# Making the first residual load of GpSimd wait for the first inverse rows

## The chip, the cores and the metric

One core of one Trainium2 chip. The metric is the device time of the kernel in microseconds, launch to end; a traced execution also has a span, about 1.8 us shorter. Two executions of the kernel before were in a slower state (207.19 us in the first set of runs, 206.88 us in a later one) and are left out where fast runs are compared.

## The reference

```python
xn = layernorm(x)                                   # x: 1 x 2048 x 640, bfloat16
s  = irfft2(rfft2(xn) * (w_r + 1j * w_i))           # spectral filter over rows and columns
g  = silu((gelu(xn @ w_gate) * (xn @ w_up)) @ w_down)   # inner width 1536
out = x + s * g
```

The last line matters here: it adds x again, the *residual*, at the very end, when the x that was loaded at the start has been overwritten.

## The kernel before

The kernel is one long list of tasks that a planner in Python puts in order for each engine before the program is built. TensorE carries both halves: the transforms as matmuls, and the gated network, whose matmuls fill the gaps while the spectral data goes through DRAM. Each engine takes its list in order (VectorE's 320 and ScalarE's 224 operations come in one order in every trace whose lists are the same), and waits come only from data dependencies. Four parts matter.

The forward rows. Two slabs of rows at a time (a pair j, of eight) are transformed, evicted by ScalarE into a tile `mc`, which has two buffers, and stored to DRAM:

```python
BUFS = dict(..., mc=2, ..., xr=3, ...)
...
def cp(e, s=s, pa=pa):
    if s == 0:
        place(A, (2, D))                              # A is a buffer of mc
    copy_on(e, A.tile[:, s, :], flat(pa.tile)[:, 0:D])
...
stored[j] = dma(lambda: D2[:, 2 * j:2 * j + 2, :], lambda: A.tile, (0, -1, j), 327680, after=outs, ...)
```

The gate, whose GELU shares ScalarE's queue with those evictions, and whose PSUM bank `pg` (two of them) is free for TensorE only after it:

```python
nc.scalar.activation(out=ge.tile, in_=pg.tile ..., func=ACT.Gelu_apprx_tanh)
```

The residual loads, 16 of 160 KB, issued by GpSimd into a tile `xr` with three buffers:

```python
def load_res(n1):
    sx = Slot("xr")

    def go(e):
        place(sx, (D,))
        nc.gpsimd.dma_start(out=sx.tile, in_=xv[:, n1, :])
    xr_in[n1] = sx, add(go, "POOL", (600, 600), (5, n1), after=[y_done[n1]], new=[sx], size=163840)
```

And their only reader, VectorE, at the end of each slab: `res = yg + xr`, in the trace the operation `res<-yg,xr`.

`after=[y_done[n1]]` is a statement to the planner only. The load does not touch the inverse rows `y`, so no wait is built for it: on the chip it goes out as soon as GpSimd gets there and a buffer of `xr` is free.

## Time and profile before

| | before |
|---|---|
| median, three runs | 204.23 us (203.73 to 207.19) |
| span of the trace | 202.6 us |
| TensorE busy | 195.1 us, 96% |
| first three residual loads | issued at 48.69 us, first used at 154.97 us |
| store of the sixth pair of forward rows | issued at 50.60 us, ScalarE released at 57.88 us |

In the timelines below a line is: start in us, duration in us, engine, line of the program, operation, output<-input, shapes, count, and in brackets the idle time before it and what ended it. Such lines are taken from ScalarE's and TensorE's timelines of the kernel before:

```profile
57.88 1.29 ACT L296 CAST mc<-sp 128x640 bf16<-128x640 f32 x2 [4.82 <-DMA D<-mc]
...
59.72 1.24 PE L886 MATMUL pg<-xnT,Wg 128*128 128x512 bf16 x5 [1.35 <-ACT ge L903]
```

The two evictions stand idle for 4.82 us until the store out of their buffer is done, and the gate matmuls behind them in turn for 1.35 us.

TensorE's order is the same in all versions (its 1527 weight loads come in the same order in every trace). From the start of its last forward matmul to the start of its first spectral one lie the same instructions, and the stop lies in between:

```profile
52.54 0.38 PE L532 MATMUL sp<-mb,F1T 128*128 128x512 bf16 x1
...
67.28 1.06 PE L670 MATMUL sp<-T,BU 128*128 128x128 bf16 x16
```

I call 67.28 - 52.54 = 14.74 us stretch 1. In the same way stretch 2 goes from there to the first inverse matmul (78.03 us), and stretch 3 from there to the last block of inverse matmuls (43.59 us). What remains at the end, from the last VectorE operation to the end of the program, I call the tail (2.7 us; it is given to a tenth, as the span is).

### The profile page before, as it was taken

How to read it: one execution, taken by the hardware profiler on the slowest of the kernel's cores; microseconds unless marked ns; L12 is line 12 of the kernel's file. 1: busy time of each engine (PE TensorE's matmuls, PEld its weight loads, DVE VectorE, ACT ScalarE, POOL GpSimd, SP SyncE). 2: the span in 40 equal slices, each digit the busy share in tenths (PEclk: the TensorE clock that was granted, in tenths of full speed). 3: DMA queues.
4: the chain of work that ended last, by engine and by line, in shares of the span. 5: the costliest groups of instructions: out<-in, count | busy, mean ns of one | idle time of the engine just before them, and what ended most of it. 6: DMA issues, size and time to landing. Idle time of an engine off the chain costs nothing.

```text
span 202.6 us, 4105 instructions
## 1 busy us (share of the span) xinstructions
PE 195.1 (96%) x1509; PEld 117.9 (58%) x1527; DVE 149.6 (74%) x320; ACT 127.0 (63%) x224; POOL 33.0 (16%) x72
## 2 busy tenths in 40 slices
PE   7999999999979999999999999999999999999992
PEld 2994444666534646677755555467765555556771
DVE  3689979999323229999998999942247798888774
ACT  4898997965343567778766775433366666766421
POOL 2413347598000000000000000000001122111210
PEclk9999999999999999999999999999999999999998
DMA  6999999569966968643243201106800333323431
GB/s 178 328 316 326 347 391 231 119 160 222 178 246 198 345 183 233 138 122 113 68 130 104 96 5 60 68 13 218 351 3 32 99 119 110 98 100 97 129 102 65
DMA packets 35894, 32.62 MB, mean 161 GB/s; under 512 B 10910, under 2 KB 32930, under 8 KB 35874
## 3 DMA queue, kind: packets, MB, share of 16 engines
q1 hardware_dynamic: 34434, 29.49, 49.2%
q0 software_dynamic: 1152, 2.66, 5.3%
q10 hardware_dynamic: 288, 0.20, 0.5%
q8 instruction: 12, 0.20, 0.4%
q14 instruction: 8, 0.07, 0.1%
HBM read 22.51 MB, written 9.19 MB: 156 GB/s over the span
## 4 chain that ended last, share of the span: by engine, by line
PE 92%; DMA 4%; issue 1%; ACT 1%; DVE 1%; DVEq 0%; ACTq 0%
PE pu L886 24%; PE pg L886 23%; PE pg L968 13%; PE pu L968 12%; DMA D<-mc 4%; PE sp L697 3%; PE sp L830 3%; PE sp L772 2%; PE sp L806 2%; PE sp L368 2%; PE sp L670 2%; PE sp L532 1%; PE sp L690 1%; PE sp L824 1%; PE sp L463 1%
## 5 line engine op out<-in xcount | busy, mean ns | idle before, releaser
L886 PE MATMUL pg<-xnT,Wg 128*128 128x512 bf16 (+1 forms) x235 | 56.2, 365 | 1.8 <-ACT ge L903 1.4
L886 PE MATMUL pu<-xnT,Wu 128*128 128x512 bf16 (+1 forms) x237 | 57.2, 365 | 0.5
L907 DVE TENSOR_TENSOR uT<-pu,ge 128x512 bf16<-128x512 f32 x46 | 31.6, 689 | 22.6 <-PE pu L886 15.3
L968 PEld LDWEIGHTS <-uT 128*128 128x128 bf16 x396 | 37.8, 98 | 13.6
L903 ACT ACTIVATE ge<-pg 128x512 bf16<-128x512 f32 x46 | 27.3, 597 | 23.3 <-PE pg L886 22.4
L886 PEld LDWEIGHTS <-Wg 128*128 128x128 bf16 x285 | 25.5, 99 | 23.6 <-issue 1.6
L886 PEld LDWEIGHTS <-Wu 128*128 128x128 bf16 x285 | 25.1, 98 | 21.8
L931 POOL DMA_DIRECT2D xr<-in_A_x_dram x16 | 8.8, 551 | 135.7 <-DVE res L955 135.7
L968 PE MATMUL pg<-Wd,uT 128*128 128x320 bf16 (+2 forms) x204 | 30.5, 293 | 0.0
L968 PE MATMUL pu<-Wd,uT 128*128 128x320 bf16 (+1 forms) x192 | 29.7, 297 | 0.0
L296 ACT CAST ma<-sp 128x644 bf16<-128x644 f32 (+1 forms) x32 | 23.4, 793 | 9.7 <-PE sp L830 7.9
L296 ACT CAST mc<-sp 128x640 bf16<-128x640 f32 x15 | 9.8, 694 | 6.1 <-DMA D<-mc 4.8
L296 ACT CAST IU<-sp 128x640 bf16<-128x640 f32 x16 | 10.9, 691 | 4.2 <-PE sp L772 4.1
L977 ACT ACTIVATE th<-pg 128x320 f32<-128x320 f32 (+2 forms) x17 | 7.3, 427 | 9.9 <-PE pg L968 8.9
L296 ACT CAST Vt<-sp 128x640 bf16<-128x640 f32 x16 | 10.8, 691 | 3.7 <-PE sp L806 3.7
L982 DVE SCALAR_TENSOR_TENSOR G<-th,pg 128x320 bf16<-128x320 f32 (+1 forms) x16 | 7.6, 478 | 7.1 <-ACT th L977 6.9
L977 ACT ACTIVATE th<-pu 128x320 f32<-128x320 f32 (+1 forms) x16 | 7.0, 438 | 9.2 <-PE pu L968 9.0
L982 DVE SCALAR_TENSOR_TENSOR G<-th,pu 128x320 bf16<-128x320 f32 (+1 forms) x16 | 7.7, 479 | 5.6 <-ACT th L977 5.3
L433 POOL TENSOR_TENSOR RSTD<-MVA,mh 128x1 f32<-128x1 f32 x12 | 8.7, 729 | 4.0 <-DVE MVA L415 3.2
L848 DVE TENSOR_TENSOR mb<-ma 128x640 bf16<-128x640 bf16 x8 | 3.9, 493 | 7.0 <-ACT ma L296 7.0
L750 DVE TENSOR_TENSOR R<-Y 64x644 bf16<-64x644 bf16 x16 | 7.8, 490 | 0.4
L418 ACT ACTIVATE th<-X 128x640 bf16<-128x640 bf16 x11 | 8.1, 732 | 0.0
(106 smaller groups left out, 245.7 us busy)
## 6 DMA issues: line engine op xcount, KB each, us to landing
BU<-D SPq DMA_DIRECT2D x8, 640.0 KB
D<-mc SPq DMA_DIRECT2D x8, 320.0 KB
xr<-in_A_x_dram POOLq DMA_DIRECT2D x16, 160.0 KB, 2.6
D<-IU SPq DMA_DIRECT2D x8, 320.0 KB
out_dram<-res SPq DMA_DIRECT2D x15, 160.0 KB
Wg<-in_B_w_gate_dram SPq DMA_DIRECT2D x6, 320.0 KB
Wu<-in_B_w_up_dram SPq DMA_DIRECT2D x6, 320.0 KB
Wd<-in_B_w_down_dram SPq DMA_DIRECT2D x6, 320.0 KB
```

The source lines that it names most:

```text
L296: return nc.scalar.copy(out=out, in_=in_) if e == "ACT" else nc.vector.tensor_copy(out=out, in_=in_)
L418: nc.scalar.activation(out=place(junk, (D,)), in_=x, func=ACT.Copy, scale=-1.0 / D, accum_out=less)
L433: nc.gpsimd.tensor_tensor(out=rstd, in0=var, in1=mh, op=ALU.pow)
L697: nc.tensor.matmul(into(q, ri), lhsT=sZ.tile[:, q, ri, :], rhs=FM[:, kinds[q][2] + (4 if ri and kind == 0 else 0), :], start=False, stop=T ...
L750: nc.vector.tensor_tensor(out=o, in0=Yf[:, ::-3, :], in1=Yf[:, 1:3, :], op=ALU.subtract)
L886: nc.tensor.matmul(ps.tile[:, lo:hi + more], lhsT=w[:, c, t * P:(t + 1) * P], rhs=XR[:, c, lo + (lo > 0):hi + 1 if lo or more else hi] if ...
L903: nc.scalar.activation(out=ge.tile, in_=pg.tile if src is None else src, func=ACT.Gelu_apprx_tanh)
L907: nc.vector.tensor_tensor(out=u.tile, in0=pu.tile if src is None else src, in1=ge.tile, op=ALU.mult)
L931: nc.gpsimd.dma_start(out=sx.tile, in_=xv[:, n1, :])
L968: nc.tensor.matmul(ps.tile[:, 0:hi - lo], lhsT=uT[grp, ks[i]].tile[:, j * P:(j + 1) * P], rhs=Wd[:, ks[i], lo:hi], start=(i == 0), stop=(i ...
L977: nc.scalar.activation(out=th.tile[:, 0:hi - lo], in_=ps.tile[:, 0:hi - lo], func=ACT.Tanh, scale=0.5)
L982: nc.vector.scalar_tensor_tensor(out=G2.tile[:, lo:hi], in0=th.tile[:, 0:hi - lo], scalar=1.0, in1=ps.tile[:, 0:hi - lo], op0=ALU.add, op1 ...
```

## The change

Its intent is to keep the three early loads out of the busy time of the DMA engines. One element of the first inverse rows is copied into the buffer that the load will overwrite. The copy has to wait for those rows, the load has to wait for the copy, and GpSimd holds all later loads behind them (after the change they start at 151.02 us and later).

```diff
         def go(e):
             place(sx, (D,))
+            if n1 == 0:
+                nc.gpsimd.tensor_copy(out=sx.tile[0:1, 0:1], in_=y_of[0].tile[0:1, 0, 0:1])
             nc.gpsimd.dma_start(out=sx.tile, in_=xv[:, n1, :])
-        xr_in[n1] = sx, add(go, "POOL", (600, 600), (5, n1), after=[y_done[n1]], new=[sx], size=163840)
+        xr_in[n1] = sx, add(go, "POOL", (600, 600), (5, n1), after=[y_done[n1]], new=[sx], use=[] if n1 else [y_of[0]], size=163840)
```

## The prediction

> **What bounds the kernel now.** I read the page first. TensorE is busy 195.1 of 202.6 us, at a granted clock of nine tenths or more in every slice but the last, so the program is bound by its matmuls and a change can win only what TensorE still idles, about 7.5 us, or lose by making it idle more.
>
> ```profile
> PE 195.1 (96%) x1509; PEld 117.9 (58%) x1527; DVE 149.6 (74%) x320; ACT 127.0 (63%) x224; POOL 33.0 (16%) x72
> L931 POOL DMA_DIRECT2D xr<-in_A_x_dram x16 | 8.8, 551 | 135.7 <-DVE res L955 135.7
> L296 ACT CAST mc<-sp 128x640 bf16<-128x640 f32 x15 | 9.8, 694 | 6.1 <-DMA D<-mc 4.8
> ```
>
> The second line is the group that the change touches: 16 residual loads of GpSimd. It idles 135.7 us ahead of them, which costs nothing in itself. The third line says where a transfer stops an engine: ScalarE waits once, for 4.8 us, for a store out of the tile mc.
>
> Next, the view of TensorE's waits, to place its idle time. Only two are left: 1.2 us at the very start, for the dummy operand of the warm-up, and this one:
>
> ```profile
> PE pg L886 <- ACT ge L903: 1.4, 1, 1.4
> ```
>
> With the 4.0 us after the last matmul at 198.6 us, which no load of row 0 touches, these make 6.6 of the 7.5 us. So 1.4 us is the only large item in the body. Next, the chain of waits between 46 and 62 us, to see what made it (columns: start, duration, what):
>
> ```profile
> 50.30 0.29 ACT mc L296
> 50.60 7.21 DMA D<-mc
> ...
> 58.47 0.70 ACT mc L296
> 59.17 0.51 ACT ge L903
> 59.68 0.04 issue
> 59.72 1.24 PE pg L886 x5
> ```
>
> The store of the sixth pair of forward rows is issued at 50.60 and takes 7.21 us. The tile mc has two buffers, so ScalarE cannot evict the eighth pair before this store has landed; ScalarE is in order, so the GELU behind those two evictions waits too, and TensorE runs out of free gate banks. It stops from 58.37 to 59.72, 1.35 us. Landing to restart takes 59.72 - 57.88 = 1.84 us, so TensorE would not stop at all if the store landed at 58.37 - 1.84 = 56.53 or sooner, that is 1.35 us earlier (landing read as the 57.88 at which ScalarE resumes).
>
> Last, GpSimd in time and the DMA queues. The first line is GpSimd's timeline, the next ones the queue's shares of the 16 engines between 52 and 53 us and between 52 and 56 us:
>
> ```profile
> 48.69 1.72 POOL L931 DMA_DIRECT2D xr<-in_A_x_dram  x3
> ...
> 155.75 0.55 POOL L931 DMA_DIRECT2D xr<-in_A_x_dram  x1 [105.35 <-DVE res L955]
> ```
>
> ```profile
> q0 software_dynamic: 87, 0.33, 107.9%
> q1 hardware_dynamic: 156, 0.03, 18.6%
> ```
>
> ```profile
> q0 software_dynamic: 149, 0.49, 56.0%
> q1 hardware_dynamic: 875, 0.35, 53.8%
> ```
>
> Three residual loads, as many as xr has buffers, start at 48.69 although their rows are first used at 154.97, 106 us later. They move 480 KB on the software queue q0, exactly in the stretch in which the store waits behind two transposes on the hardware queue q1. Between 52 and 53 us q0 has practically all engines and q1 hardly moves.
>
> **What the Trainium skill says.** The page "DMA: Bandwidth & Descriptors", section "Queues, rings and completion order", says that each DMA engine takes turns between the queue rows that have work, packet by packet. The trace agrees: q0 has 56.0% and q1 53.8% of the engines over the same 4 us. The same page, section "Anatomy of one DMA — SWDGE (gpsimd) path", gives a load issued by GpSimd as about 2.0 us plus bytes/436e3; for 163,840 bytes that is 2.4 us, and the trace has 2.6 us for the undisturbed loads from 155 us on, but 4.9 to 7.3 us for the first three: they were in a crowd. The page "Perfetto Trace Analysis", section "Tensor Engine Instruction (MATMUL, LD_WEIGHTS)", says that GpSimd is strictly first in, first out; the loads of rows 1 and 2 therefore stay behind that of row 0.
>
> **The change part by part.**
>
> It *adds* one GpSimd copy of one element, once. The trace has no such copy; the shortest GpSimd instructions on tiny operands are 0.10 us (fills) and 0.19 us (128x1 scalar), spaced about 0.28 us to the next dependent one, so I count 0.3 us. GpSimd has nothing to do then: cost 0.
>
> It *adds a wait*: the copy reads column 0 of the first inverse rows, so it waits for VectorE's third inverse step (L856, which ends at 151.39 + 0.49 = 151.88) or, should the dependency cover the whole tile, for the fourth (L859, 152.54 + 0.48 = 153.02). The load needs the copy because both write the same buffer.
>
> It *moves* three loads, 480 KB, from 48.69 us to about 152 us. What they free early: 56.0% of 4 us is 2.24 us of all 16 engines. Had the engines been full throughout, the store would land 2.2 us earlier. They were not: between 54.5 and 56 us the DMA rate is low and the transposes' own tail sets the pace. The full stretch from 52 to 53 us is certain, the rest partly. So 1.0 to 2.2 us, in the middle 1.6 us. TensorE can use 1.35 us at the most. I count 1.25 us.
>
> What they cost late: the wake-up after VectorE's end is about 0.29 us (res ends 155.46, GpSimd's next load 155.75). Load 0 would then be issued at 151.88 + 0.29 + 0.3 = 152.5 and land 2.6 us later at 155.1, against 154.97 when VectorE wants it: a wait of about 0.1 us. With the later release it is 153.02 + 0.6 + 2.6 = 156.2: VectorE waits 1.25 us. DMA traffic is zero between 150 and 155 us, so nothing slows these loads. Rows 1 and 2 come 0.55 us apart and are wanted at 156.66 and 162.84, so they hold nothing up for long. Does a 1.25 us stop of VectorE reach TensorE? VectorE's next up-projection product starts at 157.71; before it stand four operations of 0.4 us, so it slips to about 157.9. The bank it frees is next written by TensorE at 162.15. VectorE idles 1.4 us of each 5.8 us period (0.79, 0.17 and 0.42), so the slip is gone one period later. Cost 0.
>
> Sum: 204.23 - 1.25 = 203.0 us.
>
> **Rivals.** *Everything hidden anyway.* If the store's landing depends on the transposes rather than on engine share, removing the 480 KB brings less than 0.5 us. For it: the low DMA rate after 54.5 us. Against it: q1's small share from 52 to 53 us, at 2 us of backlog. It would give about 203.8 to 204.2 us.
>
> *The wait takes the place of the one removed.* If GpSimd's wake-up or the load were much slower (5 us or more, as in the crowd of 50 us), VectorE would hold back products for long enough to stop TensorE; 0.5 to 2 us lost, 204 to 205 us. Against it: the DMA engines are idle there and TensorE has over 3 us in hand on the bank.
>
> *A larger gain.* If the next stage, which waits for all eight stores, also started earlier in a way that TensorE feels: but TensorE shows no wait between 59.72 us and its last matmul, so it could win only fractions of the remaining 0.9 us of small gaps: 202.3 us at best.
>
> **Range and chances.** The centre is 203.0. The full gain with some small gaps closed and a lucky run gives 202.2; no gain and a median as high as that before gives 204.3. Two per cent is 4.1 us, three times the whole idle time that this change can reach, and a loss of that size would need a stop of TensorE that no step above produces. So faster 0.02, same 0.96, slower 0.02. The kernel before had one run of 207.19 among three, so a stray slow run can move a median of few runs; this is most of the 0.02 for slower.
>
> **What would show each step.** Right: GpSimd's first load starts near 151 us, after a copy; between 52 and 56 us q0 is nearly empty; the store issued near 50.6 us takes about 5.6 us instead of 7.21; ScalarE's wait for it falls from 4.8 to about 3.2 us; TensorE's wait for ge falls from 1.4 us to almost none; VectorE shows a new wait of 0.1 to 1.3 us for the load xr near 154 us, and TensorE none behind it. Wrong: the store still lands near 57.8 us; or it lands earlier and TensorE stops somewhere else, for another transfer or for VectorE after 150 us.

## The result, and the profile after

| | before | after |
|---|---|---|
| median of six runs | 204.65 us (203.73 to 207.19) | 202.78 us (202.59 to 203.32) |
| fast runs, ratio | | 0.992 (95%: 0.9894 to 0.9945) |
| span of the trace | 202.6 us | 201.1 us |
| stretch 1, 2, 3 | 14.74, 78.03, 43.59 us | 13.22, 78.03, 43.60 us |
| tail | 2.7 us | 2.7 us |
| store: issue to ScalarE's release | 7.28 us | 3.42 us |

A ratio is the mean time of one kernel's fast runs over the mean time of the other's in the same rounds, so it is not quite the ratio of the medians. The gain in these runs is 0.8%, clear of noise and within the two per cent that count as "same". The kernels further down that hold the loads back and add nothing near 50 us gain 0.4 to 0.7% over the kernel before of their own group.

The page of the kernel after: TensorE has the same work in less time, GpSimd's load group has a copy ahead of it, and ScalarE's evictions into mc idle for 2.3 us in all, no longer mostly for the store.

```profile
PE 195.2 (97%) x1527; PEld 117.4 (58%) x1527; DVE 149.7 (74%) x320; ACT 127.2 (63%) x224; POOL 33.1 (16%) x73
L932 POOL COPY xr<-s 1x1 bf16<-1x1 bf16 x1 | 0.2, 182 | 101.8 <-DVE s L856 101.8
L296 ACT CAST mc<-sp 128x640 bf16<-128x640 f32 x15 | 9.8, 694 | 2.3 <-PE sp L533 1.3
```

(The kernel before shows 1509 matmuls and this one 1527. Each of the 18 missing records leaves a hole of about 0.05 us, 0.9 us in all, which is why its "idle" adds up to more than its stops.)

Timelines of ScalarE and TensorE after: the evictions wait 0.96 us instead of 4.82, the gate matmuls that had stopped start at 58.28 without a wait, and stretch 1 is 65.83 - 52.61 = 13.22 us.

```profile
54.10 1.29 ACT L296 CAST mc<-sp 128x640 bf16<-128x640 f32 x2 [0.96 <-DMA D<-mc]
```

```profile
52.61 0.38 PE L532 MATMUL sp<-mb,F1T 128*128 128x512 bf16 x1
...
58.28 1.24 PE L886 MATMUL pg<-xnT,Wg 128*128 128x512 bf16 x5
...
65.83 1.06 PE L670 MATMUL sp<-T,BU 128*128 128x128 bf16 x16
```

GpSimd's timeline after: the copy starts right after VectorE's third inverse step (149.95 + 0.49 = 150.44 us), the first load half a microsecond later.

```profile
150.50 0.18 POOL L932 COPY xr<-s 1x1 bf16<-1x1 bf16 x1 [101.75 <-DVE s L856]
151.02 0.59 POOL L933 DMA_DIRECT2D xr<-in_A_x_dram  x1 [0.34 <-POOL xr L932]
```

VectorE's timeline after has its first residual addition at 153.67 us, right behind the product that ends at 152.92 + 0.69 = 153.61. The load had landed at 153.55 us (151.02 + 2.5). From the start of the product to the start of the addition it is 0.75 us, and was 154.97 - 154.37 = 0.60 us in the kernel before: VectorE waited about 0.15 us for the load, too little for the views to show as idle time.

```profile
152.92 0.69 DVE L907 TENSOR_TENSOR uT<-pu,ge 128x512 bf16<-128x512 f32 x1 [0.42 <-PE pu L886]
153.67 0.49 DVE L957 TENSOR_TENSOR res<-yg,xr 128x640 bf16<-128x640 bf16 x1
```

The queues after, between 52 and 53 us (packets, MB, share of 16 engines): the hardware queue alone, at full share, where it had 18.6% before.

```profile
q1 hardware_dynamic: 345, 0.35, 111.9%
```

### The profile page after: what moved, and what is told of

Same layout as the page of the kernel before. It is cut to its first block, busy times and chain, and to the rows that moved or that the text cites.

```text
span 201.1 us, 4125 instructions
## 1 busy us (share of the span) xinstructions
PE 195.2 (97%) x1527; PEld 117.4 (58%) x1527; DVE 149.7 (74%) x320; ACT 127.2 (63%) x224; POOL 33.1 (16%) x73
## 4 chain that ended last, share of the span: by engine, by line
PE 79%; DMA 10%; SPq 4%; DVE 3%; issue 1%; ACT 1%; DVEq 0%
PE pg L886 19%; PE pu L886 19%; PE pg L970 13%; PE pu L970 12%; DMA X<-in_A_x_dram 6%; SPq L303 4%; DMA RB<-D 4%; PE sp L697 3%; PE sp L830 3%; PE sp L772 2%; PE sp L806 2%; PE sp L670 2%; PE sp L532 1%; PE sp L690 1%; PE sp L824 1%
## 5 line engine op out<-in xcount | busy, mean ns | idle before, releaser
L886 PE MATMUL pg<-xnT,Wg 128*128 128x512 bf16 (+1 forms) x245 | 57.5, 366 | 0.0
L903 ACT ACTIVATE ge<-pg 128x512 bf16<-128x512 f32 x46 | 27.4, 597 | 25.5 <-PE pg L886 25.0
L886 PEld LDWEIGHTS <-Wu 128*128 128x128 bf16 x285 | 25.1, 98 | 21.8
```

The lines of the kernel that those rows point to most:

```text
L886: nc.tensor.matmul(ps.tile[:, lo:hi + more], lhsT=w[:, c, t * P:(t + 1) * P], rhs=XR[:, c, lo + (lo > 0):hi + 1 if lo or more else hi] if ...
L903: nc.scalar.activation(out=ge.tile, in_=pg.tile if src is None else src, func=ACT.Gelu_apprx_tanh)
```

## The experiments

Theory A: the 480 KB of early residual loads slow the store out of `mc`, and through mc buffer, ScalarE and gate bank they stop TensorE; nothing else about the change matters. Twelve kernels ran, in three groups on three chips, each group beside its own runs of the kernel before, whose medians were 203.88, 204.38 and 204.37 us; so across groups it is ratios that compare. All twelve gave the right result. "Store" is from its issue to ScalarE's release, "VectorE" its longest wait for the residual rows (0: none that the views show).

| run | store | stretch 1 | stretch 3 | tail | VectorE | median | ratio to before |
|---|---|---|---|---|---|---|---|
| e1_copy_only | 5.97 | 13.22 | 43.60 | 2.7 | 0 | 203.56 | 0.9991 (0.9953 to 1.0029) |
| e2_dummy3 | 3.05 | 13.22 | 43.59 | 2.7 | 0 | 202.75 | 0.9958 (0.9923 to 0.9992) |
| e2_dummy1 | 3.95 | 13.22 | 43.59 | 2.7 | 0 | 202.86 | 0.9960 (0.9929 to 0.9991) |
| e4_before_mc3 | no wait | 13.50 | 43.60 | 2.7 | 0 | 203.10 | 0.9964 (0.9939 to 0.9990) |
| e3_early1 | 3.69 | 13.22 | 43.60 | 3.1 | 0.4 | 203.36 | 0.9956 (0.9921 to 0.9992) |
| e3_early2 | 5.02 | 13.23 | 43.59 | 3.1 | 0 | 203.53 | 0.9971 (0.9935 to 1.0007) |
| e3_early3 | 6.36 | 13.69 | 43.59 | 3.1 | 0 | 204.47 | 1.0007 (0.9972 to 1.0042) |
| e7_chain3 | 3.19 | 13.22 | 45.03 | 2.7 | 6.2 | 204.29 | 1.0000 (0.9957 to 1.0042) |
| e6_wait_zt | 3.24 | 13.22 | 43.59 | 2.7 | 0 | 202.83 | 0.9933 (0.9883 to 0.9983) |
| e8_col639 | 3.47 | 13.22 | 43.59 | 2.7 | 1.4 | 202.94 | 0.9946 (0.9910 to 0.9982) |
| e10_sp3_behind | 3.43 | 13.22 | 43.60 | 3.4 | 0 | 203.67 | 0.9977 (0.9942 to 1.0011) |
| e11_zt_mc3 | no wait | 13.22 | 43.59 | 2.7 | 0 | 202.78 | 0.9935 (0.9905 to 0.9966) |

Stretch 2 was 78.02 to 78.04 us in every one. The stretches and waits are from one traced execution each, the medians from four or six.

**e1_copy_only: the copy without the wait.**

```diff
-nc.gpsimd.tensor_copy(out=sx.tile[0:1, 0:1], in_=y_of[0].tile[0:1, 0, 0:1])
+nc.gpsimd.tensor_copy(out=sx.tile[0:1, 0:1], in_=ident[0:1, 0:1])
```

> The copy stays, its wait goes: it reads the identity matrix, ready since 1.5 us, so GpSimd's three loads go out at about 49 us as before. Theory A (the 480 KB in the crowd of 48 to 58 us are the whole cause): as the kernel before, the store out of mc takes about 7.2 us, TensorE waits about 1.4 us for ge, ratio to before 0.998 to 1.002. Rival B (the added instruction or its dependence on the buffer reorders something, and the traffic is hidden): as the changed kernel, ratio 0.992, no wait of TensorE for ge near 58 us.

The ratio is 0.9991: no gain from the copy in itself is seen. But the traced execution, at 203.01 us the fastest of its four (up to 204.55), shows no stop of TensorE at all, with the store at 5.97 us. So the stop is not there in every execution; how often it is, the record does not say, as each kernel has one trace (that the kernel before is about 1.6 us slower in the mean than the changed one suggests a stop in most). The limit of the prediction explains it: the kernel before would not have stopped had ScalarE been released by 56.53 us, which is 3.99 us after its last forward matmul at 52.54. Here that matmul was at 52.73, the limit is 56.72, and the release came just inside it:

```profile
56.55 1.29 ACT L296 CAST mc<-sp 128x640 bf16<-128x640 f32 x2 [3.29 <-DMA D<-mc]
```

**e2_dummy3 and e2_dummy1: dummy loads that missed their moment.** The changed kernel with three (one) more loads ahead of the copy, into the memory of a table that is loaded only at 75 us.

```diff
             if n1 == 0:
+                for i in range(3):
+                    nc.gpsimd.dma_start(out=flat(TI)[:, i * D:i * D + D], in_=xv[:, i, :])
                 nc.gpsimd.tensor_copy(...)
```

> The changed kernel with three dummy loads of the same 160 KB each, from the same rows, issued by GpSimd at the old moment into a tile that is still unused then; the real loads keep their wait. Theory A: the stop comes back, TensorE waits about 1.4 us, store near 7.2 us, ratio to before 0.998 to 1.002. Rival B (what helps is the later moment of the real loads, for buffers or VectorE): ratio 0.992.

> The same with one dummy load of 160 KB. Theory A with a cost in proportion to bytes: the store, 3.4 us without them and 7.2 us with three, takes about 4.7 us, it lands before TensorE's limit of 56.5 us, no wait of TensorE, ratio 0.992. Rival C (any load of the software queue stalls the transposes, whatever its size): the store takes 6 us or more and TensorE waits 0.5 to 1.4 us, ratio 0.995 to 1.0.

These did not test what they were to test: this place in the program comes after the readers of the table, so the dummies waited for them and ran at 100 to 133 us. They serve as a control. Up to 480 KB more through GpSimd, at a quiet time, cost nothing: stretch 2, in which they ran, is 78.03 us in both, and the medians are 202.75 and 202.86 us. (The ratios are 0.996 because this group's kernel before was faster. The trace of e2_dummy3 is the slowest of its four, 203.83 us; its extra 1 us lies before stretch 1, whose first matmul starts at 53.57 us.)

**e4_before_mc3: cure the wait, leave the loads.** The kernel before, with the eighth pair evicted into the memory of that table instead of the second mc buffer. (A real third buffer does not fit into SBUF: with `mc=3` the program does not build.)

```diff
-                if s == 0:
+                if s == 0 and j == 7:
+                    A.tile = flat(TI)[:, 0:2 * D].rearrange("p (s d) -> p s d", s=2)
+                elif s == 0:
                     place(A, (2, D))
```

> The kernel before, loads where they were, with the eighth pair of forward rows evicted into a third buffer (the memory of a table that is loaded only at 75 us) instead of the second mc buffer. Theory A with the chain store, mc buffer, ScalarE, gate bank, TensorE: ScalarE no longer waits for the store, TensorE's wait of 1.4 us is gone though the store still takes about 7 us; ratio 0.992 to 0.994. Rival D (the load traffic reaches TensorE by another way too, or the late store delays the next stage): ratio 0.996 to 1.0, with a new wait of TensorE near 60 to 68 us.

ScalarE's wait for the store and TensorE's wait for the bank are gone, which shows that the path through the mc buffer is real. But stretch 1 is 13.50, not 13.22 us. The loads are still in the crowd, the stores land late, and the regrouped rows that the spectral stage reads are issued only at 62.12 us (before: 61.49; after the change: 57.70). TensorE now waits for them, seen in the timeline of its weight loads:

```profile
66.33 0.73 PEld L672 LDWEIGHTS <-BU 128*128 128x128 bf16 x13 [0.60 <-DMA BU<-D]
```

So rival D is right in part: behind the first path stands a second one, shorter in what it costs (13.50 - 13.22 = 0.28 us), which emptying the crowd also clears.

**e3_early1, e3_early2, e3_early3: the traffic put back, in doses.** The changed kernel, with one, two or three dummy loads issued by GpSimd at the old moment, this time ahead of the table's own load.

```diff
-lambda e, ri=ri, w=w: nc.gpsimd.dma_start(out=D4[15:16, 1, ri, L:LP], in_=w[0:1, 0:1])
+lambda e, ri=ri, w=w: [nc.gpsimd.dma_start(out=D4[15:16, 1, ri, L:LP], in_=w[0:1, 0:1])]
+    + [nc.gpsimd.dma_start(out=flat(TI)[:, i * D:i * D + D], in_=xv[:, i, :]) for i in range(3 * ri)]
```

> One dummy load of 160 KB at about 48.7 us. Theory A with cost in proportion to bytes: store out of mc 4.3 to 5 us (3.4 without, 6 to 7.2 with three), lands before TensorE's limit, no stop, ratio 0.992 to 0.995. Rival C (any load of the software queue in this stretch upsets the transposes): store 6 us or more, TensorE stops in part, ratio 0.996 to 1.0.

> Two dummy loads at about 48.7 us; the store out of mc released ScalarE at 54.1 us with none of them, 54.5 with one, 57.1 with three. Theory A with a cost that grows faster than the bytes (two loads overlap with more of the transposes): release at 55 to 56.5 us, just ahead of TensorE's limit, no stop or a small one, the stretch of TensorE from the last forward matmul to the first spectral one 13.2 to 13.4 us (13.22 without a stop, 13.69 with three loads in their profile, 14.74 in the kernel before); ratio 0.993 to 0.998. Rival (proportional): release at 54.8 to 55.2 us.

> The three dummy loads of e2_dummy3, now put into the program ahead of the table's own load, so that GpSimd issues them at about 48.7 us (in e2_dummy3 they waited for the table's readers and ran at 100 to 133 us, which cost nothing). The real loads keep the wait. Theory A (bytes in the crowd): software queue busy between 51 and 56 us again, the store out of mc takes 6 to 7.5 us, ScalarE waits 3 to 5 us for it, TensorE stops for up to 1.5 us; ratio to before 0.997 to 1.002. Rival B (the later moment of the real loads is what helps): ratio 0.992 to 0.995, no stop.

The store took 3.69, 5.02 and 6.36 us, against 3.42 in the changed kernel: the first 160 KB cost 0.27 us, the next 1.33 and the last 1.34. The steps are rough, since each is one execution: with three loads of this size at this moment the store took 5.97 (e1_copy_only), 6.36 and 7.28 us (the kernel before) in three traces. And without early loads of GpSimd it took 3.05 to 3.95 us in seven traces, so the 0.27 us of the first load are within that scatter. That two and three loads lengthen the store is clear, the shape of the growth is not. With three loads the stop is back, and the time is that of the kernel before (1.0007), though the tail has a part in it. ScalarE's and TensorE's timelines of e3_early3:

```profile
57.09 1.29 ACT L296 CAST mc<-sp 128x640 bf16<-128x640 f32 x2 [3.77 <-DMA D<-mc]
...
58.93 1.24 PE L887 MATMUL pg<-xnT,Wg 128*128 128x512 bf16 x5 [0.31 <-ACT ge L904]
```

Its last forward matmul starts at 52.79, so its limit is 56.78 us and the release is 0.31 us late: exactly the idle time shown. Stretch 1 grew by 13.69 - 13.22 = 0.47 us.

One caution. All three have a tail of 3.1 us instead of 2.7, part of the time without being part of the question. The traces place the extra 0.4 us: it passes between two closing instructions of SyncE, after the last data have landed; why, I did not find out. Compared among themselves the tail cancels: the medians of three loads and of one differ by 204.47 - 203.36 = 1.1 us. That all of it is the stop is not shown: of the 0.8 us between the two traces, 0.47 lie in stretch 1 and 0.28 before it.

**e7_chain3 and e8_col639: how late may the loads be?** In e8 the copy reads a column that VectorE writes one step later; in e7 a chain of three tiny loads stands in the copy's place.

```diff
-nc.gpsimd.tensor_copy(out=sx.tile[0:1, 0:1], in_=y_of[0].tile[0:1, 0, 0:1])
+nc.gpsimd.tensor_copy(out=sx.tile[0:1, 0:1], in_=y_of[0].tile[0:1, 0, 639:640])      # e8
+for i in range(3):                                                                     # e7
+    nc.gpsimd.dma_start(out=sx.tile[0:1, 0:1], in_=y_of[0].tile[0:1, 0, 0:1])
```

> The copy reads column 639, which VectorE's fourth step writes about 1.1 us later than column 0. The real loads go out about 1.1 us later; VectorE waits about 1 us for the first residual rows near 154 us; TensorE, with more than 3 us in hand there, does not stop; ratio 0.991 to 0.995, as the changed kernel. Rival (any wait of VectorE reaches TensorE): its last stretch, 43.60 us from the first inverse matmul to the last, grows by 0.5 to 1 us.

> The one-element copy replaced by three one-element loads in a row on the software queue, each waiting for the one before, about 2 us each: the real loads go out some 6 us later than in the changed kernel, near 157 us. VectorE is expected to wait 5 to 6 us for the first residual rows near 154 us. Theory A's slack (TensorE has over 3 us in hand on the up-projection bank, not 6): TensorE stops 1 to 3 us once, near 160 us, ratio 0.998 to 1.006. Rival E (VectorE catches up, no loss): ratio 0.992 to 0.995.

In e8 VectorE waits 1.7 us in two pieces and TensorE's stretch 3 does not grow. In e7 the three tiny loads delay the real ones by 2.8, 1.8 and 1.9 us, VectorE waits 6.18 us, and TensorE stops once. VectorE's and TensorE's timelines of e7:

```profile
159.65 0.49 DVE L958 TENSOR_TENSOR res<-yg,xr 128x640 bf16<-128x640 bf16 x1 [6.18 <-DMA xr<-in_A_x_dram]
...
162.00 1.24 PE L886 MATMUL pu<-xnT,Wu 128*128 128x512 bf16 x5 [1.28 <-DVE uT L907]
```

Stretch 3 grew by 45.03 - 43.59 = 1.44 us, about what the change had won in stretch 1, and the ratio is 1.0000. So VectorE has about 6.2 - 1.4 = 4.8 us in hand before TensorE feels it (an estimate, as the slack need not be used up in one piece).

**e6_wait_zt: out of the crowd, but early.** The copy waits for a spectral eviction near 70 us. (The cut leaves out two arguments of the planner, the new operand and a size of 0 for this load; in the program that comes of it one residual addition of VectorE stands ahead of the product next to it.)

```diff
-nc.gpsimd.tensor_copy(out=sx.tile[0:1, 0:1], in_=y_of[0].tile[0:1, 0, 0:1])
+nc.gpsimd.tensor_copy(out=sx.tile[0:1, 0:1], in_=zt[0][0].tile[0:1, 0, 0, 0:1])
-after=[y_done[n1]]
+after=[y_done[n1]] if n1 else [zt[0][1]]
```

> The copy waits for the first spectral eviction (near 68 us) instead of the first inverse rows. Theory A (only being out of the crowd of 48 to 58 us counts): the loads go out near 68 us, no stop of TensorE at 58 us, VectorE waits for no residual rows; ratio 0.992 to 0.995, as the changed kernel. Rival F (480 KB disturb the next stage, whose tables and weights load from 60 to 90 us): a new stop of TensorE between 66 and 85 us, ratio 0.996 or more.

The loads went out at 71.07 us; ratio 0.9933, all stretches as in the changed kernel, no wait of VectorE. The three loads took 3.5, 5.3 and 6.2 us to land, so they stood in traffic here too, but no engine was stopped by it. Released at 71, 151 or 152 us, the loads leave TensorE's three stretches the same.

**e10_sp3_behind: the same bytes, queued behind the store.** Three dummy loads on SyncE's hardware queue, right after the seventh store (the cut leaves out the planner's arguments).

```diff
 nc.sync.dma_start(out=D2[:, 2 * j:2 * j + 2, :], in_=A.tile)
+for i in range(3 * (j == 6)):
+    nc.sync.dma_start(out=flat(TI)[:, i * D:i * D + D], in_=xv[:, i, :])
```

> Three dummy loads of 160 KB as in e3_early3, but on the hardware queue of SyncE, issued right behind the seventh store (about 53 us). Theory A refined (what hurts is taking turns with the transposes and the store, not the bytes as such): the sixth store, ahead of them in the same queue, still takes about 3.4 us, no stop at 58 us, ratio 0.992 to 0.996. Rival (bytes anywhere near share the engines all the same, or they delay the eighth store and the regrouping that the spectral stage reads): the store takes 5 us or more, or TensorE waits for the regrouped rows near 66 us; ratio 0.997 or more.

By its ratio, 0.9977, the rival would have won, and it would be wrong: the store took 3.43 us and all three stretches are those of the changed kernel. The excess is in the tail, 3.4 us: SyncE again pauses 0.4 us between two closing instructions, and it has more waits left to pass after the one for the last output. The same 480 KB are harmless to the store when they stand behind it in its own queue, though they run close to it (the queue is at full share until 57 us). This run changed two things at once, the queue and the moment (52.66 instead of 48.9 us), so it does not say which of the two protects the store.

**e11_zt_mc3: both cures.** e6_wait_zt with the buffer of e4_before_mc3.

> The wait at 70 us of e6_wait_zt with the third buffer of e4_before_mc3: no engine waits for the store, VectorE waits for no residual rows. Theory A: nothing is left to win there, TensorE's three stretches 13.22, 78.03 and 43.60 us as in the changed kernel; ratio to before 0.991 to 0.995. Rival (some gain is left in the store's wait): below 0.991.

202.78 us, ratio 0.9935: as the changed kernel's 0.992, within the intervals (they were compared through the kernel before, not side by side). No version is seen to beat the changed kernel; with no stop left in stretch 1, nothing more is seen to win on this path.

## Why the prediction was right, point by point

- **The bound and the place of the gain.** Right. All of the gain is in stretch 1; stretches 2 and 3 did not move by more than 0.01 us.
- **What TensorE can use: 1.35 us.** Too small by 0.17 us. Stretch 1 shrank by 14.74 - 13.22 = 1.52 us, while the idle time read 1.35. A group of matmuls is recorded with 1.24 us and started every 1.08 us: with matmuls flowing, the next record starts 0.16 us before the last one ends. A stop loses that overlap too. e3_early3 repeats it, 0.31 us idle and 0.47 us lost. The Trainium skill, page "Perfetto Trace Analysis", section "Tensor Engine Instruction (MATMUL, LD_WEIGHTS)", says that TensorE's end times are estimated by the profiler, not observed, which fits.
- **The store earlier by 1.0 to 2.2 us, ScalarE's wait down to about 3.2.** Mis-sized. The store came 7.28 - 3.42 = 3.86 us earlier and the wait fell to 0.96. My term counted only the software queue's own share of the engines. The shares of the DMA queues show the rest. Before, from 50 to 58 us:

```profile
q1 hardware_dynamic: 1943, 1.44, 79.8%
q0 software_dynamic: 177, 0.49, 28.4%
```

  After, from 50 to 55 us:

```profile
q1 hardware_dynamic: 1973, 1.53, 106.3%
```

  The software queue held 28.4% of 8 us = 2.27 us. But the hardware queue, too, held the engines for 79.8% of 8 = 6.38 us before, and 106.3% of 5 = 5.32 us after, for slightly more bytes. Together that is 2.27 + 1.06 = 3.33 of the 3.86 us (roughly, as a share above 100% means that packets overlap in time). The 1.06 us are all in packets of up to 300 bytes: in the same two windows there were 1415 and 1416 of them, with a mean of 33.9 ns before and 21.8 ns after, while the packets above 1.5 KB took 3.14 and 3.12 us of the 16 engines. The size of this term did not reach the time, since TensorE could use no more than its stop. Why the small packets took longer is open; the other queue alone need not be the reason, since in e10_sp3_behind, with the loads in the same queue, their mean between 50 and 56 us was 31.3 ns. So the right total has luck in it: the store's term was less than half of what it should be, and the limit of what TensorE could use hid that.
- **"The trace agrees" with turn-taking by packet.** It does not show it. Equal shares over 4 us need no turns, and between 52 and 53 us, with work in both queues, the shares were 107.9% and 18.6%: the software queue's data packets were 5120 bytes and took 266 ns in the mean, those of the hardware queue about 200 bytes and 19 ns. The kept records do not say which DMA engine moved a packet, so turns can be neither confirmed nor denied.
- **1.25 us counted as the gain.** The traces show 1.52 us less in stretch 1 and 0.07 us lost before it, which makes the 202.6 - 201.1 = 1.5 us of the spans. The stop varies between executions, as e1_copy_only shows; the ratio of all fast runs, 0.992, is about 1.6 us. The late-load kernels of the other groups (ratios 0.9933 to 0.9960) won 0.8 to 1.4 us, so the record bears out a gain near 1.25 us, but no finer figure.
- **The late side: cost 0.** Right. The copy waited for VectorE's third step, as the first of my two cases had it; the load went out at 151.02 us (predicted: near 151) and VectorE waited about 0.15 us for it (predicted: about 0.1). Two terms were wrong and cancelled, which is luck: the wake-up took 0.06 us and not 0.29, and from the copy's start to the load's it was 0.52 us and not 0.3. e8_col639 shows that the second case would have cost TensorE nothing either.
- **The rivals.** "Everything hidden anyway" fell with e3_early3 and e1_copy_only. "The wait takes the place" exists, but only from about 5 us of VectorE's wait on (e7_chain3). "The next stage" was not felt in the kernel before, because the bank stopped TensorE first; e4_before_mc3 uncovered it. The 0.9 us of small gaps that "A larger gain" wanted to draw on were not idle time but the holes of the 18 missing records.

## What to carry to other kernels

A load with nothing to wait for goes out as soon as its queue reaches it, and may meet the one transfer that an engine is waiting for; a one-element copy from data that is ready at a better time is a cheap way to hold it, and at the three moments tried between the crowd and the use (71, 151 and 152 us) the exact one did not matter to TensorE. When a transfer holds up an engine, work out the latest landing that would not stop the bound engine: here this limit told which traced executions stop, and in e3_early3 by how much. And compare stretches of the bound engine between fixed instructions, not only whole times: e10_sp3_behind would have been misread because of a longer end of the program.

## What the Trainium skill lacked or had wrong

- "DMA: Bandwidth & Descriptors", section "Issuing engines are not separate DMA queues", says that DMAs of any engine interleave on the same 16 engines. It lacks that it matters for a single transfer where the others stand: with 480 KB issued ahead of it on the other queue the store took 6.36 us, with the same bytes issued behind it in its own queue 3.43 us (queue and moment were changed together, so which of them matters is not shown).
- The same page, "Queues, rings and completion order", tells of taking turns, not of a price: with the early loads in the software queue, the hardware queue held the engines for 6.38 us with 1.44 MB, without them for 5.32 us with 1.53 MB, and its packets of up to 300 bytes took 33.9 against 21.8 ns in the mean (25.5 ns in e3_early3; one trace each).
- The same page's fit for a load issued by GpSimd gives an estimate of 2.4 us for 160 KB and the undisturbed loads took 2.6 us; in the crowd they took 4.9 to 7.3 us. The fit has no term for other traffic.
- "Perfetto Trace Analysis" lacks that a stop of TensorE costs more than the idle time shown: 1.35 us idle were 1.52 us, 0.31 us idle were 0.47 us.
- No page has that the end of a program can differ by a pause of SyncE between its closing instructions: in four runs, those with dummy loads near 50 us, about 0.4 us passed there, and the tail was 3.1 to 3.4 us instead of 2.7. Whether the loads cause it is not shown.
